# Attention into a gated feed-forward product, one core: weight parts remade from stored raw columns, block sums begun three items ahead, attention in 128-row pieces

## The chip, the cores and the metric

The kernel runs on one core of one Trainium2 chip, as one program. The core has five engines that run side by side and are ordered only by semaphores: PE multiplies matrices, DVE and POOL work element by element, ACT copies, casts and evaluates functions, and SP issues the DMAs, one after the other from one queue, which 16 DMA engines then carry out. PE writes to PSUM, where the tiles lie in eight banks; POOL doesn't read them. The metric is the device time of one execution in microseconds (us), lower is better. The time before is the median of three runs.

## The reference

For each of 8 batches and 8 heads, keys and values are averaged over groups of 8 rows, 576 queries attend to the 72 pooled keys, and the joined heads go through a product of two linear maps and a third:

```python
k_p = k.reshape(B, H, Sp, pool, D).mean(axis=3)      # B, H, S, D = 8, 8, 576, 64; pool 8, Sp = 72
v_p = v.reshape(B, H, Sp, pool, D).mean(axis=3)
scores = scale * np.matmul(q, k_p.transpose(0, 1, 3, 2))
scores = scores - np.max(scores, axis=-1, keepdims=True)
attn = np.exp(scores)
attn = attn / (np.sum(attn, axis=-1, keepdims=True) + 1e-09)
attn_out = np.matmul(attn, v_p)
x = attn_out.transpose(0, 2, 1, 3).reshape(B * S, H * D)          # 4608 x 512
out = ((x @ w_a) * (x @ w_b)) @ w_out                             # 512 -> 1536 -> 512
```

## The kernel before

**High and low parts.** Every factor of a matrix product is split in two: a high part, which is an ACT cast to a shorter format, and a low part, which is what the cast lost, a subtraction on DVE or POOL (`low_part`, L250). A product is then three matmuls, high x high, high x low and low x high. So each split costs one ACT cast and one subtraction, and `either` lets the subtraction go to DVE or to POOL, whichever the planner finds free first.

**Tokens.** The 4608 rows are six pairs of 768, each pair two halves of 384. Attention for a pair must be done before its feed-forward starts. A batch has 576 rows, so that batches end in the middle of halves.

**Attention in pieces.** `chunks_of` cuts each batch by itself into pieces, four of 128 rows and one of 64: 40 pieces. For a piece, `chunk` loads the queries (from the second half on into a `tmp` slot `q`), splits them (`qh`, `ql`), multiplies them with the pooled keys `kdiag` of the piece's batch (matmuls `psc`), subtracts the maximum, takes the exponential, divides by the sum `z`, splits the weights (`pr`, `rem`), transposes them on PE with an identity as moving operand (`ptr`, L836), and copies them out (`turned`, `rest`). Pieces below number `SUMMED` (those of the first two pairs) take scores in three matmuls of 144 columns (L755); the rest in one of 288 and one of 144 (L774, L777). When all pieces of a block (the rows of one batch in one half) are there, `po` matmuls multiply them with the pooled values `vdiag`.

**Feed-forward.** The 1536 hidden columns are 12 groups f of 128, taken in twos j. The first pair is done plainly (`normal`, items "n"): half 0 with j = 0 and 1 alone, then both halves with j = 2 to 5, then half 1 with j = 0 and 1. `ps` matmuls (banks XA, XB, YA, YB) multiply the two weight matrices with the split operands `x`; ACT copies the one product (`h`), DVE multiplies the other onto it, ACT and DVE or POOL split the result (`hh`), and `acc` matmuls multiply it with `w_out`. The other five pairs are items "s" (`block`, one for each j): seven products in the manner of Strassen, with combinations S1 to S4 of the weight blocks (`block_sums`) and T1 to T4 of the operands (`prepare`). The first half of the program until the first "s" item is called the opening here.

**Where weights come from.** In the opening `convert_weights` joins each weight from two 32-bit words (ACT twice, DVE once), as raw columns `raw` for `w_a` and `w_b` and `o` for `w_out`. `split_inner` and `split_outer` split them (`own`, `wo`). Raw columns are stored to DRAM (`kept_raw`, 512 KB for each f); so are the split parts of f 0 to 3 (`kept` from `own`, eight of 512 KB) and the split `w_out` of every f (`kept_o`, 12 of 512 KB). When the plain items come to j = 0 and 1 for the second time, `load_parts` and `load_outer` load these parts again. `block_sums` loads raw columns, makes and stores S1 to S4 (and the split blocks of f from 4 on) two items ahead of their use in pair 1; later pairs load all parts from DRAM.

**Buffers.** `own`, `wo`, `load`, `raw`, `raw2`, `sum` and more share 15 slots of 4 KB for each partition, with a quota for each kind (`QUOTA`); the small tiles share 4 `tmp` slots; `h` has 7 buffers and `hh` 6.

**The order.** No order is written by hand. The class `Machine` plays the whole program through with a cost for each instruction: tasks are generators that ask for an engine or wait for a condition, an engine that is free takes the request with the lowest rank (due times of items and pieces; the products of `inner` come last with 2e4, `outer` with 1e4), and what it takes is issued at once. So each engine's order is fixed when the program is built, and each engine then keeps to it: an instruction that waits holds up all behind it on that engine. Any change of a quota, a due time or a count shifts the order of everything behind.

## Time and profile before

| | |
|---|---|
| median of 3 runs | 1042.36 us (1041.38 to 1043.06) |
| the profiled execution | 1041.39 us |
| its span, first to last instruction | 1039.6 us |
| mean granted TensorE clock | 0.985 |
| PE matmuls, DVE, ACT, POOL instructions | 5424, 1231, 1004, 222 |
| moved by DMA | 230.63 MB, mean 222 GB/s |

The span is 1.8 us shorter than the execution that it belongs to, and that execution lies 1.0 us below the median. A view by stages is the most useful one here, since the opening and the later pairs have different limits. "Busy" is the time in which an engine worked on at least one instruction; matmuls overlap each other, so that a row's mean duration is longer than the distance from one matmul to the next.

### The profile page before, as it was taken

The page shows a single profiled execution, that of the slowest core. Times are in us where ns is not written, and L with a number is a line of the kernel's source. Part 1 is how long each engine was busy: PE and PEld are TensorE (multiplying, and loading weights), DVE is VectorE, ACT ScalarE, POOL GpSimd, SP SyncE. Part 2 cuts the span into 40 slices and gives each one's busy share as a digit, 9 for nine tenths or more (in the row PEclk, how much of TensorE's full clock was granted, in tenths as well). Part 3 has the DMA queues.
Part 4 walks back from the last instruction along what each step waited for, and adds up shares of the span by engine and source line. Part 5 has one row for each costly group of instructions (what it writes and reads, how often), then busy time and mean ns, then how long its engine had stood idle before and what let it go on. Part 6 is the DMA issues. An engine that isn't in the chain of part 4 may idle for free.

```text
span 1039.6 us, 15076 instructions
## 1 busy us (share of the span) xinstructions
PE 992.2 (95%) x5424; PEld 914.4 (88%) x5424; DVE 717.6 (69%) x1231; ACT 470.9 (45%) x1004; POOL 261.8 (25%) x222
## 2 busy tenths in 40 slices
PE   4789799999999999999999999999999999999998
PEld 3678799999889998999998999998899999899997
DVE  7997587477778889757767668669866665634444
ACT  4877686334654455543334354334354334232111
POOL 4353000135444356211116010104210112210000
PEclk9998899999999999999999999999999999999999
DMA  9787874548756676846743768554674645576521
GB/s 332 240 288 247 308 246 158 184 155 304 286 190 224 251 253 258 329 159 242 288 172 133 276 210 315 199 173 170 234 287 172 213 167 182 193 290 212 192 82 61
DMA packets 76426, 230.63 MB, mean 222 GB/s; under 512 B 12288, under 2 KB 12288, under 8 KB 76352
## 3 DMA queue, kind: packets, MB, share of 16 engines
q1 hardware_dynamic: 76352, 229.67, 62.7%
q8 instruction: 43, 0.70, 0.3%
q14 instruction: 31, 0.25, 0.1%
HBM read 184.55 MB, written 45.09 MB: 221 GB/s over the span
## 4 chain that ended last, share of the span: by engine, by line
PE 85%; DVE 6%; ACT 3%; issue 2%; DMA 2%; POOL 1%; POOLq 0%; SPq 0%; ACTq 0%; DVEq 0%
PE acc_s L1195 8%; PE acc_s L1197 8%; PE acc_s L1196 8%; PE psXB L1120 4%; PE psXB L1122 4%; PE psXB L1121 4%; PE psXA L1120 4%; PE psXA L1121 4%; PE psXA L1122 4%; PE psYA L1120 3%; PE psYA L1122 3%; PE psYA L1121 3%; PE psYB L1120 3%; PE psYB L1121 3%; PE psYB L1122 3%; PE ptr L836 3%
## 5 line engine op out<-in xcount | busy, mean ns | idle before, releaser
L1224 DVE TENSOR_TENSOR y<-acc_s,y 128x512 f32<-128x512 f32 x150 | 102.5, 689 | 74.6 <-PE acc_s L1197 73.5
L1195 PE MATMUL acc_s<-wo,hh 128*128 128x512 f32 x360 | 145.8, 405 | 1.9 <-ACT hh L1076 1.9
L1197 PE MATMUL acc_s<-wo,hh 128*128 128x512 f32 x360 | 142.8, 397 | 0.4 <-POOL hh L250 0.4
L1196 PE MATMUL acc_s<-wo,hh 128*128 128x512 f32 x360 | 142.4, 396 | 0.0
L1076 ACT CAST hh<-h 128x384 fp32r<-128x384 f32 x144 | 73.8, 514 | 86.5 <-DVE h L1165 52.0
L250 POOL TENSOR_TENSOR hh<-h,hh 128x384 fp32r<-128x384 f32 x41 | 42.9, 1047 | 271.9 <-ACT hh L1076 235.1
L1147 ACT COPY h<-psXA 128x384 f32<-128x384 f32 x90 | 43.0, 478 | 136.4 <-PE psXA L1122 136.2
L250 DVE TENSOR_TENSOR hh<-h,hh 128x384 fp32r<-128x384 f32 x103 | 67.8, 661 | 27.7 <-ACT hh L1076 26.7
L1197 PEld LDWEIGHTS acc_s<-wo,hh 128*128 128x128 f32 x360 | 67.9, 189 | 17.6 <-POOL hh L250 0.8
L1195 PEld LDWEIGHTS acc_s<-wo,hh 128*128 128x128 f32 x360 | 68.2, 189 | 15.2 <-ACT hh L1076 2.6
L1196 PEld LDWEIGHTS acc_s<-wo,hh 128*128 128x128 f32 x360 | 68.4, 190 | 12.5
L787 ACT ACTIVATE weights<-weights 128x576 f32<-128x576 f32 (+1 forms) x40 | 27.5, 688 | 97.3 <-DVE weights L718 97.3
L796 POOL TENSOR_TENSOR weights<-weights,z 128x576 f32<-128x576 f32 (+1 forms) x24 | 28.4, 1181 | 142.2 <-DVE z L791 132.7
L843 ACT CAST turned<-ptr 128x512 fp32r<-128x512 f32 (+1 forms) x80 | 41.5, 547 | 37.4 <-PE ptr L836 37.3
L1165 DVE TENSOR_TENSOR h<-h,h 128x384 f32<-128x384 f32 x69 | 52.9, 768 | 1.9
L733 DVE TENSOR_REDUCE weights<-psc 128x144 f32<-128x288 f32 (+1 forms) x104 | 43.5, 448 | 12.2 <-PE psc L777 12.2
L1120 PE MATMUL psXB<-xT,load 128*128 128x384 f32 x148 | 50.6, 342 | 0.0
L1120 PE MATMUL psXA<-xT,load 128*128 128x384 f32 x148 | 50.1, 338 | 0.0
L1122 PE MATMUL psXB<-xT,load 128*128 128x384 f32 x148 | 49.7, 336 | 0.0
L1121 PE MATMUL psXB<-xT,load 128*128 128x384 f32 x148 | 49.7, 336 | 0.0
L1121 PE MATMUL psXA<-xT,load 128*128 128x384 f32 x148 | 49.7, 336 | 0.0
L1122 PE MATMUL psXA<-xT,load 128*128 128x384 f32 x148 | 49.7, 336 | 0.0
(322 smaller groups left out, 2885.5 us busy)
## 6 DMA issues: line engine op xcount, KB each, us to landing
load<-kept_S SPq DMA_DIRECT2D x96, 512.0 KB, 4.9
load<-kept SPq DMA_DIRECT2D x86, 512.0 KB, 4.7
wo<-kept_o SPq DMA_DIRECT2D x64, 512.0 KB, 4.7
kept_S<-sum SPq DMA_DIRECT2D x24, 512.0 KB, 3.3
out<-y SPq DMA_DIRECT2D x36, 256.0 KB, 2.2
q<-in_q SPq DMA_DIRECT2D x29, 256.0 KB, 5.0
kraw<-in_k SPq DMA_DIRECT2D x24, 288.0 KB, 4.0
kept_o<-wo SPq DMA_DIRECT2D x12, 512.0 KB, 6.1
```

The lines of the kernel that those rows point to most:

```text
L250: eng.tensor_tensor(out=lo, in0=src, in1=hi.bitcast(F32), op=ALU.subtract)
L733: nc.vector.tensor_reduce(out=s[:n, 2 * g:2 * g + 2, :], in_=pt[:n, :2 * hk].rearrange("p (w h s) -> p h s w", w=2, h=2), axis=AX.X, op=AL ...
L1076: yield on_act(HB, lambda: nc.scalar.copy(e[:, 0], h))
L1120: nc.tensor.matmul(pt, w[:, 0, mat, c], xo[:, 0, kk], start=(opens and kk == 0), stop=False, **more)
L1121: nc.tensor.matmul(pt, w[:, 0, mat, c], xo[:, 1, kk], start=False, stop=False, **more)
L1122: nc.tensor.matmul(pt, w[:, 1, mat, c], xo[:, 0, kk], start=False, stop=(kk == 1), **more)
L1147: yield on_act(HB, lambda: nc.scalar.copy(t, pt))
L1165: yield either(HB, lambda eng: eng.tensor_tensor(out=t, in0=t, in1=a, op=ALU.mult))
L1195: nc.tensor.matmul(pt, e[:, 0, cs], w[:, 0], start=(y == 0), stop=False)
L1196: nc.tensor.matmul(pt, e[:, 0, cs], w[:, 1], start=False, stop=False)
L1197: nc.tensor.matmul(pt, e[:, 1, cs], w[:, 0], start=False, stop=(y == 1))
L1224: yield on_dve(DM, lambda: nc.vector.tensor_tensor(out=acc[row], in0=pt, in1=acc[row], op=ALU.add))
```

## The change

Pieces are now 128 rows each over all 4608 rows, without regard to batches: 36, three to a half. A piece that straddles two batches (number 4, 13, 22 and 31) has its first 64 rows from one and the rest from the other. Its `qh` and `ql` get 64 columns of zeros in the middle (POOL, `clear`), so that two sets of score matmuls, one for each batch's `kdiag`, add up in the same bank. `turned` is now one tile for each half in place of one for each block, and `values_of` multiplies a block's part of it. `SUMMED` becomes 12, still the first two pairs.

Split parts are no longer stored in the opening. `split_again` loads raw columns of f 0 to 3 and splits them again for the plain items that come to j = 0 and 1 a second time. `split_outer` stores raw columns of `w_out` (`kept_ro`, 256 KB) in place of the split ones; `outer_again` loads and splits them again, 4 for those plain items and 12 for pair 1, and stores the latter split (`kept_o`) for the later pairs. `block_sums` begins three items ahead, makes the split blocks of f 0 to 3 too (12 to 18 stores of them), and has 9 `sum` and 4 `raw2` slots; `h` has 6 buffers. New in all are 30 casts, each with its subtraction: 6 of split blocks in `block_sums`, 8 in `split_again` and 16 in `outer_again`.

```diff
-def chunks_of(b):
-    sizes = [128, 128, 128, 128, 64] if b % 2 == 0 else [64, 128, 128, 128, 128]
...
+NCHUNK = B * S // P
+PER_HALF = HB // P
+
+def parts_of(i):
+    out, t = [], i * P
+    while t < (i + 1) * P:
+        n = min((i + 1) * P, (t // S + 1) * S) - t
+        out.append((t // S, t - i * P, n))
+        t += n
     return out
...
-TMP_QUOTA = {"o": 1, "q": 2, "kv": 1}
+TMP_QUOTA = {"o": 2, "q": 2, "kv": 1}
...
-SUMMED = 14
+SUMMED = 4 * PER_HALF
-QUOTA = {"early": 10, "raw": 2, "words": 3, "own": 4, "wo": 4, "load": 7, "raw2": 3, "sum": 6, "T2": 1}
+QUOTA = {"early": 10, "raw": 2, "words": 3, "own": 4, "wo": 4, "load": 7, "raw2": 4, "sum": 9, "T2": 1}
...
-    gates = Slots(sb, "h", 7, {"h": 7})
+    gates = Slots(sb, "h", 6, {"h": 6})
...
-            parts[f, h] = e
-            if f < 2 * LEAD:
-                keep("own", (f, h), e, 1e4 + f)
+            parts[f, h, 0] = e
...
-        tmps.give("o", f)
-        parts["o", f] = e
-        keep("wo", ("o", f), e, 1e4 + f)
+        loaded_o[f] = "wo", f, e
+        def store():
+            kept["raw o", f] = dr.tile([P, 512], F32, name=f"kept_ro_{f}")
+            yield transfer(kept["raw o", f], w, 1 << 18)
+            tmps.give("o", f)
+            mark("kept", "raw o", f)
+        start(due_f[f] + 4, store())
+
+    def split_again():
+        yield lambda: (NF - 1, 1, 0) in parts
+        for f in range(2 * LEAD):
+            yield lambda: ("raw", f) in kept and slots.can("raw2")()
+            r = slots.take("raw2", ("again", f), [P, 2, 512], F32)
+            yield transfer(r.rearrange("p m c -> p (m c)"), kept["raw", f], 1 << 19)
+            for h in range(2):
+                yield slots.can("own")
+                e = slots.take("own", (f, h), e_shape, F32R)
+                src = r[:, :, h * 256:(h + 1) * 256]
+                yield on_act(512, lambda: nc.scalar.copy(e[:, 0], src))
+                yield low(512, e[:, 1], src, e[:, 0])
+                parts[f, h, 1] = e
+            slots.give("raw2", ("again", f))
+        mark("split again")
+
+    def spare_for(kind):
+        return lambda: slots.can(kind)() and (("split again",) in done or len(slots.free) > 3)
+
+    def outer_again():
+        for x in range(NF, NF + 2 * LEAD + NF):
+            f = x - NF if x < NF + 2 * LEAD else x - NF - 2 * LEAD
+            yield until(("kept", "raw o", f))
+            yield lambda: at_item[0] >= NJ - 1 and next_o[0] == x
+            yield spare_for("wo") if x >= NF + 2 * LEAD else slots.can("wo")
+            next_o[0] += 1
+            e = slots.take("wo", x, [P, 2, 512], F32R)
+            yield tmps.can("o")
+            w = tmps.take("o", x, tmp_shape, F32)
+            yield transfer(w, kept["raw o", f], 1 << 18)
+            yield on_act(512, lambda: nc.scalar.copy(e[:, 0], w))
+            yield low(512, e[:, 1], w, e[:, 0])
+            tmps.give("o", x)
+            loaded_o[x] = "wo", x, e
+            if x >= NF + 2 * LEAD:
+                keep("wo", x, e, 1e4 + x, False, ("o", f))
...
-        yield lambda: at_item[0] >= first_s + j - 2
+        yield lambda: at_item[0] >= first_s + j - 3
...
-        if j >= LEAD:
-            yield from split((2 * j, 0), r1[:, :, left])
-            yield from split((2 * j, 1), r1[:, :, right])
+        yield from split((2 * j, 0), r1[:, :, left])
+        yield from split((2 * j, 1), r1[:, :, right])
...
+        gap = P // 2 if len(parts) > 1 else 0
+        qh = sb.tile([P, NK, P + P // 2], F32R, tag="qh", name=f"qh_{i}", bufs=1)
+        ql = sb.tile([P, NK, P + P // 2], F32R, tag="ql", name=f"ql_{i}", bufs=1)
...
+        by_batch = [(b, kdiag[b % 2], slice(x * gap, x * gap + P)) for x, (b, _, _) in enumerate(parts)]
...
-                yield until(("keys", b, g0))
+                yield until(*(("keys", b, g0) for b, _, _ in by_batch))
...
+                        todo = [(qq, w, kd, cs) for _, kd, cs in by_batch for qq, w in ((qh, 0), (qh, 1), (ql, 0))]
```

Three places of the engines' orders, before and after. In these rows the number in a name counts tiles, and shapes are partitions x elements of what is written.

SP, the DMA queue, in the opening; the profile before has these rows issued between 51.9 and 63.2 us. Before:

```order
L247 DMA words_o<-in_wo 128x1024
L247 DMA kept_1_336<-own_22_317 128x1024
L247 DMA words_12_107<-in_wb 128x1024
L247 DMA q_12_617<-in_q 128x512
L247 DMA kept_raw_337<-raw_first 128x1024
L247 DMA kept_o_453<-wo_24_404 128x1024
L247 DMA q_14_687<-in_q 128x512
L247 DMA kept_0_427<-own_23_394 128x1024
L247 DMA words_a<-in_wa 128x1024
```

And now:

```order
L252 DMA kept_raw_360<-raw_first 128x1024
L252 DMA kept_raw_506<-raw_first 128x1024
L252 DMA q_10_548<-in_q 128x512
L252 DMA kept_ro_605<-o_7_331 128x512
L252 DMA words_11_106<-in_wa 128x1024
L252 DMA q_13_642<-in_q 128x512
L252 DMA words_13_108<-in_wo 128x1024
L252 DMA kraw_0_665<-in_k 128x576
L252 DMA kraw_1_666<-in_k 128x576
```

The stores of `own` and the split `wo` between the loads of words are gone; the stores of raw columns stand there alone, those of `w_out` half as wide.

PE, at the first products of the feed-forward, where the first batch ends. Before:

```order
L1047 MATMUL psXB_0_471<-xB_0_385,own_21_274 128x384
L1048 MATMUL psXB_0_471<-xB_0_385,own_21_274 128x384
L836 MATMUL ptr_0_482<-ident,pr_437 128x128 x4
L755 MATMUL psc_0_488<-kdiag_72,qh_423 64x144 x2
L755 MATMUL psc_0_488<-kdiag_72,ql_424 64x144
L755 MATMUL psc_0_488<-kdiag_72,qh_423 64x144 x2
L755 MATMUL psc_0_488<-kdiag_72,ql_424 64x144
L1046 MATMUL psXB_0_471<-xB_0_386,own_22_317 128x384
```

And now, directly behind the matmuls of `psXA` and ahead of those of `psXB`:

```order
L1105 MATMUL psXA_0_443<-xB_0_385,own_22_332 128x384
L819 MATMUL psc_0_463<-kdiag_72,qh_422 128x144 x2
L819 MATMUL psc_0_463<-kdiag_72,ql_423 128x144
L819 MATMUL psc_0_463<-kdiag_73,qh_422 128x144 x2
L819 MATMUL psc_0_463<-kdiag_73,ql_423 128x144
L819 MATMUL psc_0_463<-kdiag_72,qh_422 128x144 x2
L819 MATMUL psc_0_463<-kdiag_72,ql_423 128x144
L819 MATMUL psc_0_463<-kdiag_73,qh_422 128x144 x2
L819 MATMUL psc_0_463<-kdiag_73,ql_423 128x144
```

The piece of 64 rows has become the straddling piece 4, which reads the keys of both batches (`kdiag_72` and `kdiag_73`) and stands ahead of `psXB` as a whole.

ACT, in the plain item that comes to j = 1 a second time, shortly ahead of pair 1. Before:

```order
L456 CAST sum_78_2317<-sums_2303 128x512
L927 CAST xT_1_2313<-xraw_1254 128x768
L927 CAST xT_1_2338<-xraw_1254 128x768
L456 CAST sum_80_2359<-sums_2303 128x512
L1076 CAST hh_21_2383<-h_21_2300 128x384
L1087 COPY h_22_2393<-psYA_1_2364 128x384
```

And now:

```order
L462 CAST own_81_2318<-raw_0_79_2257 128x512
L1133 CAST hh_21_2331<-h_21_2291 128x384
L484 CAST wo_80_2306<-o_31_2307 128x512
L462 CAST own_83_2341<-raw_0_79_2257 128x512
L1144 COPY h_22_2351<-psYA_1_2320 128x384
L507 CAST sum_85_2376<-sums_1966 128x512
```

The casts that remake `own` and `wo` now stand between those that take the products out of PSUM.

More of the change, by code (lines that the diff above doesn't have):

```diff
@@ L86, in __init__ @@
         self.now, self.count = 0.0, 0
-        self.queues = {e: [] for e in ("PE", "DVE", "ACT", "POOL", "SP")}
+        self.queues = {e: [] for e in ("PE", "ACT", "DVE", "POOL", "SP")}
         self.free = dict.fromkeys(self.queues, 0.0)
@@ L429, in split_outer @@
         yield until(("weight", "o", f))
-        yield lambda: slots.can("wo")() and order_o[next_o[0]] == ("own", f)
+        yield lambda: slots.can("wo")() and next_o[0] == f
         next_o[0] += 1
-        e = slots.take("wo", ("own", f), [P, 2, 512], F32R)
+        e = slots.take("wo", f, [P, 2, 512], F32R)
         w = rawt.pop(("o", f))
@@ L440, in block_sums @@
     def block_sums(j):
         left, right = slice(0, 256), slice(256, 512)
-        yield lambda: at_item[0] >= first_s + j - 2
+        yield lambda: at_item[0] >= first_s + j - 3
         r = []
         for f in (2 * j, 2 * j + 1):
-            yield lambda: ("raw", f) in kept and slots.can("raw2")()
+            yield lambda: ("raw", f) in kept and spare_for("raw2")()
             r.append(slots.take("raw2", f, [P, 2, 512], F32))
@@ L453, in split @@
         def split(name, src):
-            yield slots.can("sum")
+            yield spare_for("sum")
             e = slots.take("sum", name, e_shape, F32R)
@@ L768, in chunk @@
             for g in range(NK):
-                yield until(("keys", b, g - g % 2))
+                yield until(*(("keys", b, g - g % 2) for b, _, _ in by_batch))
                 yield bank_there
@@ L819, in chunk @@
         mark("probs", i)
[L821 to L828 removed]
+        half = half_of[i]
+        c0 = (i % PER_HALF) * P
+        if c0 == 0:
+            yield until(("valued", half - 1))
+            both = sb.tile([P, 2, NK, HB], F32R, tag="turned", name=f"turned_{half}", bufs=1)
+            turned[half] = both[:, 0], both[:, 1], sb.tile([P, NG, HB], F32R, tag="rest", name=f"rest_{half}", bufs=1)
         def turn(x, pt):
@@ L852, in chunk, with values_of @@
         mark("turned", i)
-        yield until(*(("placed", c, x) for c in members if c <= i for x in range(3)))
-        if i != members[-1]:
-            return
+        yield until(*(("placed", c, x) for c in range(i - i % PER_HALF, i + 1) for x in range(3)))
+        for j, block in enumerate(blocks):
+            if block[4] == i:
+                yield from values_of(j, rank)
+        if i % PER_HALF == PER_HALF - 1:
+            mark("valued", half)
+            del turned[half]
+    def values_of(j, rank):
+        hf, b, at, total, _ = blocks[j]
+        p = hf // 2
         yield until(("values", b))
-        hf, p = half_of[i], pair_of[i]
-        end = at + n
         if p == 0:
@@ L912, in have @@
     def have(half):
-        return until(*(("x", block_of[i]) for i in range(len(flat)) if half_of[i] == half))
+        return until(*(("x", j) for j, block in enumerate(blocks) if block[0] == half))
     def prepare(p):
@@ L964, in attn_moe_kernel @@
         kind, _, j = item
-        if kind == "n" and not own_parts(item):
-            wanted += [(2 * j + y, h) for y in range(2) for h in range(2)]
-        elif kind == "s":
+        if kind == "s":
             names = {"A11": (2 * j, 0), "A12": (2 * j, 1), "A22": (2 * j + 1, 1)}
             wanted += [names.get(a, (j, a)) for a, *_ in PRODUCTS7]
-        order_o += [("own" if own_parts(item) else "o", 2 * j + y) for y in range(2)]
+        order_o += [("o", 2 * j + y) for y in range(2)]
     loaded, loaded_o = {}, {}
-    second = range(4 * LEAD, 4 * LEAD + 7 * NJ)
     taken = {"i": 0, "o": 0}
@@ L992, in load_outer @@
         for x, name in enumerate(order_o):
-            if name[0] == "own":
+            if x < 2 * (NF + LEAD):
                 continue
-            yield lambda: at_item[0] >= NJ - 1 and name in kept and slots.can("wo")() and next_o[0] == x
+            yield lambda: name in kept and slots.can("wo")() and next_o[0] == x
             next_o[0] += 1
```

174 lines of the change are left out of this document (78 added, 96 removed).

## The prediction

> **What bounds the kernel now.** I read the page first (engines, chain), then busy time cut into stages, then PE's waits in the opening, then the groups of instructions by shape that the change touches.
>
> ```profile
> span 1039.6 us, 15076 instructions
> PE 992.2 (95%) x5424; PEld 914.4 (88%) x5424; DVE 717.6 (69%) x1231; ACT 470.9 (45%) x1004; POOL 261.8 (25%) x222
> PE 85%; DVE 6%; ACT 3%; issue 2%; DMA 2%; POOL 1%; POOLq 0%; SPq 0%; ACTq 0%; DVEq 0%
> ```
>
> PE is the bound over the whole, but 15% of the chain is not PE's. The stages show where. I cut at the first product of f = 6 (130 us), at the first "s" item (247), and then at the first product of each pair (406, 565, 725, 887); columns are window, length, busy time and count of PE, PEld, DVE, ACT and POOL, granted clock, DMA share and GB/s.
>
> ```profile
> 0.00:130.00 130.00, 96.27 (x513) 86.63 (x514) 101.77 (x184) 90.72 (x195) 47.60 (x54) 0.91 0.83 283
> 130.00:247.00 117.00, 116.61 (x643) 108.48 (x642) 80.90 (x131) 59.90 (x117) 20.88 (x13) 1.00 0.59 203
> 247.00:406.00 159.00, 157.24 (x897) 145.74 (x896) 132.73 (x223) 84.96 (x187) 79.02 (x66) 1.00 0.70 250
> 406.00:565.00 159.00, 157.47 (x877) 145.18 (x876) 112.39 (x197) 67.61 (x147) 43.78 (x32) 1.00 0.64 226
> 565.00:725.00 160.00, 157.92 (x867) 146.81 (x866) 113.29 (x201) 66.18 (x145) 24.98 (x21) 0.99 0.61 218
> 725.00:887.00 162.00, 159.60 (x882) 147.09 (x883) 106.30 (x186) 65.83 (x143) 30.07 (x26) 0.99 0.58 204
> ```
>
> From 130 us on PE is idle for 0.4 to 2.4 us in each stage: only fewer or faster matmuls help there, or harm comes from new waits. In the first 130 us PE is idle for 33.7 us, DVE is busy for 101.8 (78%), ACT for 90.7, DMA engines at 0.83. That stage is a race of several engines, DVE the fullest. PE's longest waits in the first 160 us were for others' results:
>
> ```profile
> PE psc L755 <- ACT kdiag L540: 10.4, 2, 8.0
> PE psc L755 <- ACT qh L700: 5.2, 2, 4.7
> PE psXA L1046 <- ACT own L421: 3.3, 1, 3.3
> ```
>
> (us in all, times, longest.) Of these the 8.0 is the start, which the change leaves alone.
>
> **A: the opening up to 130 us.** I counted DVE's instructions in order up to its first multiplication of f = 6: 210 rows before, 192 now. Both have 1152 attention rows behind them there, in ten pieces before (two of 64 rows) and nine now.
>
> ```profile
> L790 DVE TENSOR_REDUCE z<-weights 64x8 f32<-64x584 f32 x8 | 6.0, 746 | 0.7 <-ACT weights L787 0.7
> L733 DVE TENSOR_REDUCE weights<-psc 64x144 f32<-64x288 f32 x24 | 10.1, 440 | 1.8 <-PE psc L777 1.8
> L718 DVE TENSOR_TENSOR weights<-psc,m 64x288 f32<-64x288 f32 x4 | 1.8, 450 | 0.1
> L717 DVE TENSOR_REDUCE m<-psc 64x4 f32<-64x288 f32 x4 | 1.7, 429 | 0.0
> L250 DVE TENSOR_TENSOR own<-raw,own 128x512 fp32r<-128x512 f32 x14 | 10.8, 771 | 6.0 <-ACT own L421 5.9
> L250 DVE TENSOR_TENSOR wo<-o,wo 128x512 fp32r<-128x512 f32 x5 | 4.1, 811 | 0.0
> ```
>
> Gone are 2 `z` (1.5 us), 4 `weights` from PSUM (1.8) and 4 `m` (1.7) of 64 rows, in sum 5.0 us. Five fewer `own` subtractions (3.9) and four more `wo` (3.2) give another 0.6; the five have gone to POOL, which is busy for only 47.6 of these 130 us. So DVE has 5.6 us less. The rest of the difference is work that changes sides of my mark (the third batch's values move behind it, three conversions of words ahead of it), which I leave out. SP and the DMA engines lose much more:
>
> ```profile
> kept_o<-wo SPq DMA_DIRECT2D x12, 512.0 KB, 6.1
> kept<-own SPq DMA_DIRECT2D x8, 512.0 KB, 6.4
> load<-kept SPq DMA_DIRECT2D x86, 512.0 KB, 4.7
> wo<-kept_o SPq DMA_DIRECT2D x64, 512.0 KB, 4.7
> ```
>
> 8 stores of 512 KB go and 12 become 256 KB: 7.3 MB less, 26 us at the stage's 283 GB/s, though some of the twelve are issued after 130 us. A store has no reader in the opening; it costs by holding a slot and by delaying loads behind it. So A lies between nothing (if the 5.6 us was never what PE waited for) and, above, half of PE's idle time that isn't the start, (33.7 - 8.0) / 2 = 13. I take the row that is nearest, DVE's work: **-6**.
>
> **B: the pieces after the opening.** Three more boundaries lose a piece each (the fourth lies within A). A 64-row piece has eight `pr` and two `rem` transposes, like one of 128.
>
> ```profile
> L836 PE MATMUL ptr<-ident,pr 128*128 128x128 f32 x256 | 28.1, 253 | 4.8 <-ACT pr L808 2.7 <-ACT turned L843 1.5 <-DVE pr L250 0.6
> L836 PE MATMUL ptr<-ident,rem 128*96 128x128 f32 x64 | 9.5, 232 | 0.7 <-DVE rem L250 0.4 <-ACT turned L843 0.3
> L836 PE MATMUL ptr<-ident,pr 64*128 64x64 f32 x64 | 7.4, 251 | 0.2 <-ACT turned L843 0.2
> L836 PE MATMUL ptr<-ident,rem 64*96 64x64 f32 x16 | 2.5, 239 | 0.0
> L774 PE MATMUL psc<-kdiag,qh 128*128 128x288 f32 x80 | 22.3, 321 | 0.0
> L774 PE MATMUL psc<-kdiag,qh 128*64 128x288 f32 x24 | 6.2, 295 | 0.0
> ```
>
> Busy time over count is 0.116 and 0.156 us for 64 rows, 0.110 and 0.148 for 128: two small pieces take 2 x (8 x 0.116 + 2 x 0.156) = 2.5 us, one of 128 takes 1.2. Saved: 1.3. The scores save nothing: the straddling piece issues both sets, 8 wide matmuls at 22.3/80 = 0.28 in place of 8 at 6.2/24 = 0.26, so 0.2 is given back and as much again at most for the narrow ones. Net some 1.0 for each boundary, **-3** for three; the ends are -2 and, where the second piece's exchange with other engines costs PE too, -6: a stage with seven pieces (725 to 887) is 2 to 3 us longer than one with six (406 to 565, 565 to 725).
>
> **C: the work put off.** 30 casts and 30 subtractions are new, all between 130 and 406 us.
>
> ```profile
> L421 ACT CAST own<-raw 128x512 fp32r<-128x512 f32 x18 | 11.0, 619 | 0.9 <-PE psYB L1048 0.4 <-DVE raw L408 0.4
> L250 POOL TENSOR_TENSOR own<-raw,own 128x512 fp32r<-128x512 f32 x4 | 5.4, 1360 | 47.9 <-DVE rem L250 28.7 <-ACT own L421 19.2
> ```
>
> ACT gets 30 x 0.62 = 18.6 us. The orders give DVE 16 `wo` more and 3 `own` and 2 `sum` fewer over the whole, some 9 us net, and POOL 11 `own` and 8 `sum` more, 19 x 1.36 = 26 us. What covers it: from 130 to 406 us ACT is busy for 144.9 of 276 us, DVE for 213.6, POOL for 99.9. In front of pair 1's products DVE is at 132.7 of 159 already and PE idles 1.8 us there, no more than at 112.4 of 159 in the next pair (1.5), so the first 20 us of DVE's load cost PE next to nothing. But the casts stand between those that empty PSUM (the order of ACT in the part on the change), and each can hold back a bank by 0.62 us. Bounds: nothing, and the whole of DVE's 9 us. By the row of the neighbouring pair I take **+1**.
>
> DMAs: 14 loads of `load` and 16 of `wo`, 512 KB each, go; 16 of 256 KB, 4 of `raw2` and 6 stores come. That is fewer bytes, at a DMA share of 0.59 to 0.70: nothing. Block sums three items ahead only hold slots longer: nothing, and what they hold up is in C's upper bound. Six `h` buffers in place of seven: the orders of PE in the last pair, where no attention interferes, are equal row for row, so nothing; DVE reading late could make it up to another 2.
>
> **Sum.** -6 - 3 + 1 = -8 from the profiled execution's 1041.4 (span 1039.6 and 1.8 around it) is 1033.4. That execution lies 1.0 under the median, so 1034 is what I expect of a median.
>
> **The rivals** (their times on the median's 1042.4).
>
> *The opening was held by stores and slots, not by DVE.* For it: ACT's conversion of f = 5, for which DVE then sat idle 5.6 us, and PE's wait just behind it.
>
> ```profile
> L408 DVE SCALAR_TENSOR_TENSOR raw<-raw,words_a 128x512 int32<-128x512 int32 x9 | 6.1, 683 | 5.6 <-ACT words_a L399 5.6
> 113.94 0.48 ACT L897 COPY xraw<-po 128x384 f32<-128x384 f32 x1 [0.80 <-PE po L881]
> 114.45 0.33 PE L881 MATMUL po<-rest,vrem 96*128 96x384 f32 x1
> 118.06 0.69 PE L1046 MATMUL psXA<-xB,own 128*128 128x384 f32 x1 [3.27 <-ACT own L421]
> 119.91 0.52 PE L1046 MATMUL psXA<-xB,own 128*128 128x384 f32 x1
> 120.23 0.52 PE L1047 MATMUL psXA<-xB,own 128*128 128x384 f32 x1
> 75.00:100.00 25.00, 22.22 (x122) 20.30 (x122) 18.48 (x37) 17.05 (x39) 10.40 (x10) 0.76 0.71 248
> ```
>
> After that wait PE's matmuls come 0.32 us apart (119.91 to 120.23) and the granted clock of the whole opening is 0.91; a wait that goes takes its slow stretch along. Then A is -13: 1042.4 - 13 - 3 + 1 = 1027. Against it: what ACT waited for there, ahead of the conversion, was PE's `po` (113.94), no store. Chance 0.22.
>
> The Trainium skill, TensorE: Matmul & The Clock Gate, Part 1, says that an idle window of about 3.4 us halves PE's clock until a busy one passes. The row of 3.27 us bears it out. By it the straddling piece cuts the other way: if PE waits that long between `psXA` and `psXB` for the second batch's keys, the products behind run at half speed. It changes the odds of the next rival, not my sum.
>
> *The straddling piece's wait replaces what was saved (no change).* Its scores need the split queries of both halves and both batches' `kdiag`, and stand ahead of `psXB`, with all the first products behind them. The longest such wait before, apart from the start, is 4.7 us (for `qh`); with that A falls to -1: 1042.4 - 1 - 3 + 1 = 1039.4, and up to 1042 if C is also 2 dearer. Against it: the keys' DVE work now stands ahead of `xB`, 14 rows earlier. Chance 0.14.
>
> *DVE becomes the bound of pair 1 (slower).* Place: 247 to 406 us. DVE is the fullest there, POOL at half. If the 9 us of DVE and POOL's slower subtractions (1.36 against 0.77 us each) sit in the path from PSUM to `hh`, PE waits for all of it and for a buffer of `h` besides: C is +9 + 2 and A, by the same queue of splits ahead of the first repeated items, -3. 1042.4 - 3 - 3 + 11 = 1047. It decides once PE's idle time from 130 to 406 grows by over 6 us. Chance 0.14.
>
> That the change doesn't do what it says is excluded by the orders: 36 pieces, no stores of `own`.
>
> **How the numbers follow.** My forecast has 0.5, from 1030 to 1039; the rivals 0.22, 0.14 and 0.14. The range of 8 in 10 takes in the fast rival to 1025 and most of the slow one, to 1046. A measurement of this kernel can tell about 0.2% (2 us) from no change. Faster by more: 0.5 + 0.22 and a third of the second rival (0.03) = 0.75; within: 0.11; slower: 0.14.
>
> **What would show it.** A: the first product of f = 6 near 124 us, not 130, with DVE's busy time up to it near 96. B: 360 transposes `ptr` (the four groups above have 400), and 1 us less in each later stage with a boundary. C: PE's idle time between there and pair 2 not over 4 us more than now, DVE under 145 of the pair's 159. It is wrong if the opening keeps its length (then DVE wasn't its pace), or if PE starts to wait for `h`, `hh` or a repeated `own` behind 130 us.

## The result, and the profile after

Median 1041.87 us before (4 runs, 1041.10 to 1043.06) and 1022.81 us after (4 runs, 1022.28 to 1023.55): ratio 0.982, 95% interval 0.9805 to 0.9835. The gain is 19 us; 8 were forecast, and the range ended at 1025. From the page of the profiled execution after (1022.45 us), its span, busy times and chain:

```profile
span 1020.6 us, 14956 instructions
PE 978.5 (96%) x5380; PEld 907.6 (89%) x5380; DVE 715.7 (70%) x1214; ACT 478.6 (47%) x1002; POOL 271.5 (27%) x233
PE 91%; DVE 5%; ACT 2%; issue 1%; POOLq 0%; DVEq 0%; ACTq 0%
```

PE's share of the chain rises from 85% to 91%; DMA had 2% of it and has gone. The same cut by stages, at the first product of f = 6, of the first "s" item and of pairs 2 to 5 (columns as in the prediction):

```profile
0.00:113.90 113.90, 85.87 (x477) 79.14 (x478) 97.59 (x174) 85.77 (x179) 41.39 (x50) 0.96 0.80 266
113.90:233.30 119.40, 119.40 (x664) 111.83 (x663) 81.36 (x134) 67.55 (x138) 38.12 (x27) 1.00 0.46 160
233.30:390.80 157.50, 154.24 (x868) 143.02 (x866) 139.83 (x228) 90.64 (x191) 74.96 (x62) 1.00 0.78 275
390.80:548.40 157.60, 157.20 (x885) 146.85 (x885) 110.47 (x192) 67.84 (x145) 45.24 (x38) 1.00 0.64 231
548.40:707.10 158.70, 155.93 (x861) 144.91 (x861) 113.33 (x198) 66.81 (x144) 23.88 (x19) 1.00 0.61 220
707.10:867.00 159.90, 157.95 (x876) 146.56 (x877) 102.43 (x179) 63.58 (x134) 31.77 (x28) 0.99 0.59 207
```

In the first row, the opening up to the first product of f = 6, PE is idle for 28.0 us (113.90 - 85.87) where it was 33.7, and its granted clock is 0.96 where it was 0.91. PE's busy time in it falls too, by 10.4 us (96.27 to 85.87). Some 7 of these are the clock's, by an estimate from the two rows: 0.09 x 130.0 = 11.7 us were lost to it before, 0.04 x 113.9 = 4.6 now. So the waits that went took slow stretches along, as the rival on stores and slots had it. DVE's busy time there is 97.6 us, almost the 96 that the prediction wanted, yet the stage ends ten microseconds earlier than it wanted. The first products, in us from the span's start (the run of each part alone, e1 and e2, is told below):

| stage | before | after | e1, weights alone | e2, pieces alone |
|---|---|---|---|---|
| up to the first "s" item | 246.8 | 233.3 (-13.5) | 236.1 (-10.7) | 249.0 (+2.2) |
| pair 1 | 158.8 | 157.5 (-1.3) | 164.8 (+6.0) | 154.0 (-4.8) |
| from pair 2 to the end | 634.0 | 629.8 (-4.2) | 635.8 (+1.8) | 633.1 (-0.9) |
| sum | | -19.0 | -2.9 | -3.5 |

I compare at the first "s" item from here on: at the first product of f = 6 (129.9 and 113.9) PE has less work behind it after than before, and it does some 3 us more in the stage that follows (119.4 us busy, 116.6 before).

Where do the 13.5 us come from? The timelines of SP and ACT show one chain (start, length, engine, instruction). In the changed kernel:

```profile
77.02 0.43 SPq L252 DMA_DIRECT2D kept_raw<-raw  x1
86.89 0.33 SPq L252 DMA_DIRECT2D words<-in_wa  x1
91.73 0.62 ACT L428 CAST own<-raw 128x512 fp32r<-128x512 f32 x1
```

and before:

```profile
104.64 0.42 SPq L247 DMA_DIRECT2D kept_raw<-raw  x1
115.56 0.33 SPq L247 DMA_DIRECT2D words<-in_wa  x1
117.39 1.14 ACT L421 CAST own<-raw 128x512 fp32r<-128x512 f32 x2 [0.39 <-DVE raw L408]
```

`kept_raw<-raw` is the store of the raw columns of f = 3. Only two slots hold such columns (`raw` in `QUOTA`), so f = 5 can't be converted until that store has landed. It is issued 27.6 us earlier, the words of f = 7 follow 28.7 us earlier, and the first cast of f = 5's parts 25.7 us earlier.

### The profile page after: what moved, and what is told of

It reads as the page before. It is cut to its first block, busy times and chain, and to the rows that moved or that the text cites. A ratio compares the mean times of both kernels' runs of the same rounds, so it can differ in the third digit from the quotient of the medians.

```text
span 1020.6 us, 14956 instructions
## 1 busy us (share of the span) xinstructions
PE 978.5 (96%) x5380; PEld 907.6 (89%) x5380; DVE 715.7 (70%) x1214; ACT 478.6 (47%) x1002; POOL 271.5 (27%) x233
## 4 chain that ended last, share of the span: by engine, by line
PE 91%; DVE 5%; ACT 2%; issue 1%; POOLq 0%; DVEq 0%; ACTq 0%
PE acc_s L1248 8%; PE acc_s L1250 8%; PE acc_s L1249 8%; PE psXB L1177 4%; PE psXB L1179 4%; PE psXB L1178 4%; PE psXA L1177 4%; PE psXA L1178 4%; PE psXA L1179 4%; PE psYA L1177 3%; PE psYB L1177 3%; PE psYA L1179 3%; PE psYA L1178 3%; PE psYB L1178 3%; PE psYB L1179 3%; PE ptr L898 2%
## 5 line engine op out<-in xcount | busy, mean ns | idle before, releaser
L255 POOL TENSOR_TENSOR hh<-h,hh 128x384 fp32r<-128x384 f32 x32 | 33.0, 1033 | 267.9 <-ACT hh L1133 240.9
L255 DVE TENSOR_TENSOR hh<-h,hh 128x384 fp32r<-128x384 f32 x112 | 74.5, 670 | 29.0 <-ACT hh L1133 27.8
L860 POOL TENSOR_TENSOR weights<-weights,z 128x576 f32<-128x576 f32 x22 | 27.3, 1242 | 130.6 <-DVE z L855 126.4
L905 ACT CAST turned<-ptr 128x512 fp32r<-128x512 f32 x72 | 39.7, 589 | 29.5 <-PE ptr L898 29.4
L851 ACT ACTIVATE weights<-weights 128x576 f32<-128x576 f32 x36 | 24.8, 688 | 54.1 <-DVE weights L781 53.9
L1216 DVE TENSOR_TENSOR h<-psYA,h 128x384 f32<-128x384 f32 x60 | 33.2, 553 | 23.6 <-PE psYA L1179 22.9
L796 DVE TENSOR_REDUCE weights<-psc 128x144 f32<-128x288 f32 x96 | 40.1, 449 | 13.0 <-PE psc L843 12.8
L1177 PE MATMUL psXB<-xT,load 128*128 128x384 f32 x144 | 49.0, 340 | 0.0
L1177 PE MATMUL psXA<-xT,load 128*128 128x384 f32 x144 | 48.8, 339 | 0.0
L1179 PE MATMUL psXB<-xT,load 128*128 128x384 f32 x144 | 48.4, 336 | 0.0
L1179 PE MATMUL psXA<-xT,load 128*128 128x384 f32 x144 | 48.4, 336 | 0.0
L1178 PE MATMUL psXB<-xT,load 128*128 128x384 f32 x144 | 48.4, 336 | 0.0
```

The source lines that it names most:

```text
L255: eng.tensor_tensor(out=lo, in0=src, in1=hi.bitcast(F32), op=ALU.subtract)
L796: nc.vector.tensor_reduce(out=s[:n, 2 * g:2 * g + 2, :], in_=pt[:n, :2 * hk].rearrange("p (w h s) -> p h s w", w=2, h=2), axis=AX.X, op=AL ...
L1177: nc.tensor.matmul(pt, w[:, 0, mat, c], xo[:, 0, kk], start=(opens and kk == 0), stop=False, **more)
L1178: nc.tensor.matmul(pt, w[:, 0, mat, c], xo[:, 1, kk], start=False, stop=False, **more)
L1179: nc.tensor.matmul(pt, w[:, 1, mat, c], xo[:, 0, kk], start=False, stop=(kk == 1), **more)
```

## The experiments

Theories named in the expectations: **S**, slots held by stores until they land set the opening's pace; **D**, DVE's load does (step A of the prediction); **P**, one plan of the planner is luckier than another; **M**, the stores cost by their bytes; **Q**, they cost by their place in the queue, ahead of the store of raw f = 3; **QS**, S and Q together; **I** and **H**, on pair 1.

### The parts alone

e1_weights_only: the kernel before with the weights' part of the change (also the quotas, six buffers of `h` and the planner's new order of engines), the old pieces.

```diff
-            if f < 2 * LEAD:
-                keep("own", (f, h), e, 1e4 + f)
...
-        keep("wo", ("o", f), e, 1e4 + f)
...
+    def split_again():
...
+    def outer_again():
...
-        yield lambda: at_item[0] >= first_s + j - 2
+        yield lambda: at_item[0] >= first_s + j - 3
```

> The kernel before with the change's handling of weights (raw columns stored and split again, block sums three items ahead, quotas, six h buffers), but with the old pieces of attention. Theory S, slots: in the opening the split parts of f 0 to 3 held their slots until their stores had landed, which held up the raw columns of f = 5 and so PE: the first product of f = 6 comes at 114 to 120 us as in the changed kernel (130 before), and the whole takes 1026 to 1031. Theory D, the prediction's: DVE's load paced the opening, and most of that came off with the piece: the first product of f = 6 stays at 126 to 131, the whole takes 1038 to 1043.

Measured: 1038.33 us, 0.9962 (0.9947 to 0.9976). The first product of f = 6 comes at 116.4 us, as S had it; the time is as D had it, since what the opening gains is lost again behind it.

e2_pieces_only: the kernel before with the 128-row pieces (also six buffers of `h` and the planner's new order of engines); stores, splits and block sums as before.

```diff
-def chunks_of(b):
+def parts_of(i):
...
-SUMMED = 14
+SUMMED = 4 * PER_HALF
```

> The kernel before with the 128-row pieces (and six h buffers and the planner's new tie-break) alone; split parts stored in the opening as before. Theory S: the first product of f = 6 stays at 125 to 131 us and the whole takes 1035 to 1038, what four boundaries save on PE. Theory D: it comes at 121 to 125, the whole takes 1030 to 1034.

Measured: 1037.67 us, 0.9964 (0.995 to 0.9978). The time is as S had it, but the first product of f = 6 comes at 139.4 us, later than either theory's range. Each part alone brings 3 to 4 us, both 19. The table above shows that the opening's gain is the weights', and that alone they give 6 us of it back in pair 1. A part of that comes and goes with the clock: two of e1's ten runs took 1034.4 us at a granted clock of 0.992, the other eight 1037.5 to 1039.6 at 0.988. In e2 the wait on a slot is visible, in the timelines of ACT and DVE:

```profile
117.87 0.66 ACT L405 ACTIVATE raw<-words 128x512 f32<-128x512 f32 x1 [4.87 <-DMA kept_o<-wo]
119.11 0.69 DVE L415 SCALAR_TENSOR_TENSOR raw<-raw,words_a 128x512 int32<-128x512 int32 x1 [6.13 <-ACT words_a L406]
```

ACT's conversion of f = 5 waits 4.87 us for a slot whose split `wo` is still being stored, and DVE waits 6.13 us for ACT.

e3_tie_break: the kernel before with the planner's engines in the changed kernel's order.

```diff
-        self.queues = {e: [] for e in ("PE", "DVE", "ACT", "POOL", "SP")}
+        self.queues = {e: [] for e in ("PE", "ACT", "DVE", "POOL", "SP")}
```

> The kernel before with only the planner's order of engines at equal times changed (ACT asked ahead of DVE), as in the change: no instruction is added or removed. It measures how far the time moves when the plan is merely shuffled. S and D: within 3 us of before. Theory P, that the gain is a luckier plan: it moves by 8 us or more.

Measured: 1041.92 us, 1.0006 (0.9995 to 1.0016). That reshuffle is worth nothing.

### What the stores of the opening cost

e4_own_slots: the kernel before with six slots for own parts.

```diff
-... "own": 4, "wo": 4, "load": 7, "raw2": 3, "sum": 6, "T2": 1}
+... "own": 6, "wo": 4, "load": 7, "raw2": 3, "sum": 6, "T2": 1}
```

> The kernel before with up to six slots for split parts in the opening in place of four; stores and pieces as before. S: the fifth and sixth part needn't wait for a store, f = 5 is converted earlier, the first product of f = 6 comes 4 to 12 us earlier than at 130, the whole takes 1030 to 1038. D: no change, 1040 to 1044.

Measured: 1048.27 us, 1.0068 (1.0043 to 1.0092). S in its simple form missed, and so did D (no change). The timelines say why:

```profile
74.57 0.62 ACT L421 CAST own<-raw 128x512 fp32r<-128x512 f32 x1
...
102.56 0.42 SPq L247 DMA_DIRECT2D kept_raw<-raw  x1
...
123.78 0.64 ACT L421 CAST own<-raw 128x512 fp32r<-128x512 f32 x1
```

The parts of f = 4 are cast at 74.6 us (93.6 before), so their slots did come free. But the store of raw f = 3 still goes out at 102.6 (104.6 before), and f = 5 is later, not earlier.

e5_hold_both, e6_copy_both, e7_hold_outer, e8_hold_inner start from the changed kernel and put the stores back. e5 has both lines below, e7 the second alone, e8 the first alone; in e6 each is a copy from DRAM to DRAM of the same size and rank, for which nothing is held.

```diff
             parts[f, h, 0] = e
+            if f < 2 * LEAD:
+                keep("own", (f, h), e, 1e4 + f, False, ("u%d" % f, h))
...
         loaded_o[f] = "wo", f, e
+        keep("wo", f, e, 1e4 + f, False, ("uo", f))
```

> The changed kernel, with the stores of the opening put back that the change removed: the split inner parts of f = 0 to 3 (8 of 512 KB) and the split outer weights (12 of 512 KB), each holding its slot of the shared pool until its store has landed; nobody reads the copies. Computation on the engines is as in the changed kernel. Theory S (slots held until stores land set the pace of the opening): the first product of f = 6 goes back from 113.9 us to 122 or later, and the time to 1030 or more. Theory M (the stores cost by their bytes, 10.5 MB on the DMA engines): the same here. Theory D (DVE's lighter load set the pace): the first product of f = 6 stays within 2 us of 113.9 and the time within 2 us of 1022.8.

> The changed kernel with the same 20 transfers of 512 KB at the same ranks, but as copies from one DRAM tensor to another, so that no slot is held for them. Theory S: no more than 3 us later than the changed kernel (113.9 us at the first product of f = 6, 1022.8 us in all). Theory M: as late as the run that holds the slots, 122 us or later. Theory D: within 2 us.

> The changed kernel with only the 12 stores of split outer weights put back, slots held. Theory S, from the wait of e2_pieces_only for a slot that such a store held: it has most of the loss of the run that holds both, at least 5 us at the first product of f = 6. Theories M and D: 12 of 20 parts of the loss of both (M), nothing (D).

> The changed kernel with only the 8 stores of split inner parts put back, slots held. Theory S: the smaller part of the loss, 0 to 5 us at the first product of f = 6, with PE's waits for own parts; theory M: 8 of 20 parts of the loss of both; theory D: nothing.

Measured: e5 1034.62 us, 0.9927 (0.9912 to 0.9942); e6 1041.12, 0.9992 (0.9983 to 1.0002); e7 1023.70, 0.9821 (0.9805 to 0.9838); e8 1029.56, 0.988 (0.9865 to 0.9895). D, as the only pace, is out: no arithmetic was added in e5, and 12 of the 19 us are lost; its opening is 12.6 us longer (245.9 against 233.3 at the first "s" item). S's forecast for e6 (3 us) missed by 15. Of e7 and e8 it expected most of the loss in e7, but e7 loses 0.9 us and e8 6.8. At the mark that the expectations name, the first product of f = 6, both are late (126.2 and 123.2 us; 113.9 in the changed kernel), and only e7 makes it up by the first "s" item; so that mark says little of the time. M fits e6 but not e7, where 12 stores, 6.3 MB, cost 0.9 us. e6's timelines separate the two things that a store does:

```profile
85.81 0.62 ACT L428 CAST own<-raw 128x512 fp32r<-128x512 f32 x1
...
114.22 0.43 SPq L252 DMA_DIRECT2D kept_raw<-raw  x1
...
121.64 0.62 ACT L428 CAST own<-raw 128x512 fp32r<-128x512 f32 x1 [5.24 <-DVE raw L415]
```

With no slot held, the parts of f = 4 are as early as in the changed kernel (their second cast at 85.8; there 87.9). But the copies stand in SP's queue ahead of the store of raw f = 3, which goes out at 114.2 in place of 77.0, and f = 5 is late. Hence four runs that only move the raw stores' rank, so that they go ahead: e9_copy_behind is e6 with that edit, e10_hold_behind is e5, e11_before_raw_first the kernel before, e12_after_raw_first the changed kernel.

```diff
-        keep("raw", ("raw", f), rawt[f], 1e4 + f, f > 2)
+        keep("raw", ("raw", f), rawt[f], 9e3 + f, f > 2)
```

> As e6_copy_both (the changed kernel and 20 copies of 512 KB from DRAM to DRAM), but the stores of raw weights rank ahead of the copies (9e3 + f in place of 1e4 + f): the same bytes, another order in the queue. Theory Q (what costs is that the store of raw f = 3, which must land before f = 5 can be converted, stands behind other stores: issued at 77.0 us in the changed kernel, 104.6 before, 114.2 in e6_copy_both): that store is back before 85 us, the first product of f = 6 before 118 us, the time at 1026 or less. Theory M (bytes on the DMA engines, in whatever order): the time stays at 1036 or more.

> As e5_hold_both (20 stores of split parts, slots held), with the stores of raw weights ranked ahead of them. Theory Q: as in the run with the copies, the loss of e5_hold_both (11.8 us) goes down to 3 us or less. Theory S (the slots held by stores, not the order of the queue): the loss stays at 8 us or more, since the stores that hold slots now land later still.

> The kernel before, with the one edit that its stores of raw weights rank ahead of its stores of split parts. Nothing is removed. Theory Q in its simple form: the opening gains most of its 12 us, the time 1032 or less. Theory S, with Q only a part: the store of raw f = 3 waits for its second split, which waits for a slot of own that a store holds, so it stays near 100 us, and the time within 3 us of 1041.9.

> The changed kernel with the same edit: its only other stores of that rank come later, so nothing moves in the opening by theories Q, S and M; within 2 us of 1022.8.

Measured: e9 1027.61 us, 0.9853 (0.9829 to 0.9877); e10 1043.15, 1.001 (1.0 to 1.0019); e11 1046.08, 1.0044 (1.0029 to 1.0059); e12 1023.20, 0.9821 (0.9807 to 0.9836). The edit gives 13.5 us back where nothing is held (e6 to e9). The opening of e9 is whole again; in its profiled execution the 5 us that stay missing are lost in pair 1. They aren't the price of the bytes: one of e9's four runs took 1022.89 us, as the changed kernel does, at a granted clock of 0.995, and the other three 1027.6 to 1028.0 at 0.990. By the median e9 missed Q's 1026, though the store (83.0) and the first product of f = 6 (112.3) came as Q had them; M's 1036 is far off. The edit costs 8.5 us where slots are held (e5 to e10), against Q and as S had it, and 4 us in the kernel before, where Q expected a gain and S no more than 3 us either way. In the changed kernel it does nothing, as expected. From e9's and then from e10's timelines:

```profile
83.02 0.53 SPq L252 DMA_DIRECT2D kept_raw<-raw  x1
...
98.22 0.62 ACT L428 CAST own<-raw 128x512 fp32r<-128x512 f32 x1
```

```profile
90.20 0.62 ACT L428 CAST own<-raw 128x512 fp32r<-128x512 f32 x1
...
99.82 0.42 SPq L252 DMA_DIRECT2D kept_raw<-raw  x1
...
119.05 1.14 ACT L428 CAST own<-raw 128x512 fp32r<-128x512 f32 x2
```

In e10 the stores of split parts now land later, their slots come free later, and f = 3 itself (90.20; 72.5 in the changed kernel) waits for one; its raw columns can't be stored before they are split. A store of a split part thus delays f = 5 by two ways, and moving it in the queue trades one for the other. e13_hold_slots7 relieves both: e10 with seven slots for own parts.

```diff
-... "own": 4, "wo": 4, "load": 7, "raw2": 4, "sum": 9, "T2": 1}
+... "own": 7, "wo": 4, "load": 7, "raw2": 4, "sum": 9, "T2": 1}
```

> As e10_hold_behind (the changed kernel, 20 stores of split parts put back with their slots held, stores of raw weights ranked ahead), with up to 7 slots of the shared pool for own parts in place of 4. Theory QS (a store of a split part costs in two ways: it holds a slot that the next split needs, and it stands ahead of the store of raw f = 3, which f = 5 needs): both are relieved, so the loss of 20.3 us goes down to 6 or less, and the casts of f = 5 come before 105 us (119.0 in e10_hold_behind, 91.7 in the changed kernel). If a third thing costs (the bytes, the DMA engines' time), the loss stays at 10 or more.

Measured: 1026.51 us, 0.9848 (0.9832 to 0.9864).

```profile
82.74 0.49 SPq L252 DMA_DIRECT2D kept_raw<-raw  x1
...
100.72 0.64 ACT L428 CAST own<-raw 128x512 fp32r<-128x512 f32 x1
```

All 20 stores are there, and the first "s" item starts at 231.6 us, earlier than in the changed kernel; the 4 us that stay are lost behind it, and why stays open. What seven slots would do without the stores has no run. The runs on stores, sorted by that start (times of trace rows as above; median of the runs last):

| kernel | first cast of f = 4 | store of raw f = 3 | first cast of f = 5 | first "s" item | median |
|---|---|---|---|---|---|
| e13 | 81.9 | 82.7 | 100.7 | 231.6 | 1026.51 |
| e9 | 82.1 | 83.0 | 98.2 | 232.6 | 1027.61 |
| after | 84.7 | 77.0 | 91.7 | 233.3 | 1022.81 |
| e7 | 82.3 | 87.6 | 99.8 | 233.5 | 1023.70 |
| e8 | 83.5 | 100.0 | 110.4 | 238.9 | 1029.56 |
| e5 | 93.8 | 105.3 | 116.2 | 245.9 | 1034.62 |
| before | 93.6 | 104.6 | 117.4 | 246.8 | 1041.87 |
| e6 | 82.6 | 114.2 | 121.6 | 248.4 | 1041.12 |
| e11 | 101.6 | 101.7 | 116.0 | 249.7 | 1046.08 |
| e10 | 99.8 | 99.8 | 119.0 | 251.2 | 1043.15 |
| e4 | 74.6 | 102.6 | 123.8 | 253.7 | 1048.27 |

Wherever f = 5 is cast by 101 us, the opening is short, and nowhere else. The other runs fit: e2 and e3 cast it at 120.9 and 117.0 us and start the first "s" item at 249.0 and 246.0; e1 and e12 to e18 cast it by 101 and start between 231.6 and 236.1. A late raw store alone spoils the opening (e4, e6). A late slot was never seen alone: where the parts of f = 4 are late, so is the raw store (e5, e10, e11, before). QS holds for the changed kernel; the kernel before with both edits has no run.

### What DVE's load costs

e14_dve_open takes the sum of the exponentials twice in pieces 0 to 8; e15_dve_pair1 has `12 <= i < 19` for the condition. The order of all else stays.

```diff
             nc.vector.tensor_reduce(out=z[:n], in_=wide[:n], axis=AX.X, op=ALU.add)
+            if i < 9:
+                nc.vector.tensor_reduce(out=z[:n], in_=wide[:n], axis=AX.X, op=ALU.add)
```

> The changed kernel with the sum of the exponentials (z) taken twice in pieces 0 to 8: 9 more instructions on DVE in the opening, 9 x 0.755 = 6.8 us by the profile, the planner not told, all else in the same order. Theory D (DVE's load in the opening costs time one for one, as step A of the prediction had it): the first product of f = 6 and the time 5 to 7 us later. Theory QS: DVE has room between what it waits for; 3 us or less.

> The changed kernel with the same doubling in pieces 12 to 18, which are worked on in pair 1's stage: 7 x 0.755 = 5.3 us more on DVE, in the same order. Theory I (pair 1 with the splitting again is near DVE's limit, 140.0 of 157.5 us, so the weights' part gives back 6 us there, and the pieces pay for it by lightening DVE): 3 to 5 us later. Otherwise: 1 us or less.

Measured: e14 1026.29 us, 0.9845 (0.983 to 0.9859); e15 1025.05, 0.983 (0.9814 to 0.9847). Stages by windows, e14's opening and then e15's pair 1:

```profile
0.00:115.50 115.50, 84.98 (x476) 77.44 (x477) 100.74 (x181) 85.15 (x178) 41.84 (x50) 0.96 0.79 262
```

```profile
232.90:392.50 159.60, 154.85 (x867) 142.85 (x866) 145.59 (x234) 90.55 (x191) 76.05 (x62) 1.00 0.77 270
```

The 9 added instructions, 6.8 us by their own durations, make the opening 1.6 us longer (115.5 against 113.9 at the first product of f = 6, and the same at the first "s" item), 0.24 us for each us; 7 of them, 5.3 us, make pair 1 2.1 us longer (159.6 against 157.5), 0.4 for each. These are two executions, and both prices were measured in the changed kernel. D's 5 to 7 us are out for the opening; I is half right for pair 1. By the medians the two cost 3.5 and 2.2 us, between what the theories had. In the profiled executions (spans 1024.2 and 1024.4 us) the other 2.0 and 1.7 us come in later stages, mostly where the granted clock was at half for longer (the last section).

### Plan, buffers and block sums

e16_after_old_tie is the changed kernel with the old order of engines (e3's edit backwards); e17_weights_7h is e1 with seven buffers of `h`; e18_sums_two_ahead is the changed kernel with the block sums' old start.

```diff
-    gates = Slots(sb, "h", 6, {"h": 6})
+    gates = Slots(sb, "h", 7, {"h": 7})
```

```diff
-        yield lambda: at_item[0] >= first_s + j - 3
+        yield lambda: at_item[0] >= first_s + j - 2
```

> The changed kernel with the old order of engines in the planner, ACT and DVE exchanged, which moves instructions throughout. Theory P (a part of the gain is luck of one plan): 1026 or more. Otherwise within 3 us of 1022.8.

> e1_weights_only (the weights' part of the change, pieces as before, 6 buffers of h) with 7 buffers of h. Theory H (with splitting again in pair 1, the buffer of h that was taken away is missing there): pair 1's stage goes from 164.8 us to 160 or less and the time from 1038.3 to 1034 or less. Otherwise, if it is the load of seven pieces and the splitting together: within 2 us of 1038.3, the stage at 163 or more.

> The changed kernel with block sums begun two items ahead, as before, in place of three. By the prediction (block sums three ahead cost and bring nothing) within 2 us of 1022.8. If the early start is what keeps the sums out of pair 1's way: 3 us or more later, all of it between 233 and 391 us.

Measured: e16 1023.72 us, 0.9817 (0.9802 to 0.9831); e17 1038.34, 0.9962 (0.995 to 0.9975), pair 1 again 164.8 us; e18 1033.13, 0.9917 (0.9892 to 0.9943), four runs from 1030.02 to 1035.50. Neither the reshuffle nor the buffer matters, but the early start of the block sums does: 7.6 us by the profiled spans (1028.2 against 1020.6, both at a granted clock of 0.993), 10 by the medians; two of e18's four runs, the two slowest, had a clock of 0.988. The prediction's forecast for it, no change, is out. Pair 1 by windows in e18, e1 and e2:

```profile
231.80:395.80 164.00, 156.79 (x873) 144.80 (x872) 142.72 (x231) 89.36 (x189) 84.36 (x67) 0.99 0.76 271
```

```profile
236.10:400.90 164.80, 159.10 (x884) 145.24 (x883) 138.77 (x235) 93.11 (x200) 81.69 (x66) 0.99 0.75 265
```

```profile
249.00:403.00 154.00, 153.47 (x869) 143.69 (x868) 127.67 (x214) 83.59 (x176) 71.32 (x58) 1.00 0.72 252
```

and PE's longest waits there in e18 (us in all, times, longest):

```profile
PE psXB L1177 <- DVE h L1210: 3.9, 3, 1.9
PE acc_n L1248 <- DVE y L1277: 2.3, 1, 2.3
PE ptr L898 <- ACT turned L905: 1.0, 2, 0.8
```

Three kernels split again in pair 1: the changed one (157.5 us, POOL 75.0), e1 (164.8, POOL 81.7) and e18 (164.0, POOL 84.4), at nearly the same busy time of DVE. The two long ones have 7 to 9 us more on POOL, PE idle for 5.7 and 7.2 us in place of 3.3, and a stretch of half clock each. What splitting again costs shows over pairs 1 and 2 together, since a late pair 1 can be made up in pair 2 (from the first "s" item to the first product of pair 3): 317.8 us before and 324.1 in e1, with the old pieces and the sums early, +6.3; 314.5 in e2 and 323.8 in e18, with the new pieces and the sums late, +9.3; 314.5 in e2 and 315.1 after, with the new pieces and the sums early, +0.6. So it is nearly free only with both. That the two act through POOL is only argued from the busy times; no run changed POOL's work alone. No variant beat the changed kernel.

## Why the prediction was right or wrong

**The bound.** Right: PE over the whole, the opening the one stage with room, 13.5 of 19 us from there.

**A, -6 for DVE's lighter load: this step failed.** "I take the row that is nearest, DVE's work" priced DVE's 5.6 us one for one, and DVE wasn't what the opening waited for. With the pieces alone (e2), and so with DVE's lighter load, the opening is 2.2 us longer, not shorter. By e14 an added us of DVE costs 0.24 us there. What did make the opening faster is the removed stores, by holding no slots and by leaving the queue to the store of raw f = 3: putting them back in the two ways costs 12.6 us of the opening (e5) and 15.1 (e6), and relieving both ways with all stores in place gives it back (e13). That is the upper end of what A allowed, so the bound was right and the choice in it wrong; the rival "held by stores and slots" had the mechanism and -13.

The 5.6 us was also too large. At the mark to which the 210 rows were counted, DVE's multiplication at 146.1 us, eleven pieces lay behind it before, not ten: 1280 rows against 1152. The rows of `z` up to the marks, before and after:

```profile
L790 DVE TENSOR_REDUCE z<-weights x11: 743/753/761, 15.6 to 144.2; 128x8 f32<-128x584 f32 x9, 64x8 f32<-64x584 f32 x2
L854 DVE TENSOR_REDUCE z<-weights x9: 749/760/762, 15.5 to 110.4; 128x8 f32<-128x584 f32 x9
```

For the same rows, a piece of 128 comes for the two of 64 that go. By its rows it costs one `z` of 0.75 us and four reductions and subtractions of some 0.45, 2.6 in all, so that 3.0 of the 5.6 us are left. At e14's price they are worth 0.7 us, by an estimate that carries the price over from the changed kernel.

What spoke against the rival was misread: ACT waited for PE's `po` ahead of the conversion, "no store". But the planner plays the stores' landing through as well, and can put the conversion behind `po` because its slot comes free late; then a missing slot shows as a late place in the order, and only where the plan errs (e2's 4.87 us) as a wait. That this was its reason here follows from how the order is made; no run shows it singly. "A store has no reader in the opening" was true, and that it "costs by holding a slot and by delaying loads behind it" was said; that other stores queue behind it was not asked.

**B, -3 for the pieces.** Right in mechanism, with the size too small. The groups of transposes after count 288 + 72 = 360, as forecast, and take 42.4 us in place of 47.5, 1.3 for each boundary:

```profile
L898 PE MATMUL ptr<-ident,pr 128*128 128x128 f32 x288 | 31.6, 252 | 11.9 <-ACT pr L872 7.0 <-DVE rem L255 2.1 <-DVE weights L781 1.7
L898 PE MATMUL ptr<-ident,rem 128*96 128x128 f32 x72 | 10.8, 234 | 1.1 <-ACT turned L905 0.8 <-DVE rem L255 0.4
```

Behind the first "s" item e2 gains 4.8 + 0.9 = 5.7 us, just inside the bound of -6. In pair 1 most of it is PE's own work, 153.5 us busy against 157.2: eight pieces' transposes were in that stage before (80), six are now (60), where the sum took one less for each boundary. In the kernel before, `SUMMED` = 14 also took in the first piece of the third pair. The rest, some 1 us, is PE's idle time, with DVE at 127.7 us against 132.7.

**C, +1 for the work put off.** Alone it is +6.0 in pair 1 and +1.8 behind it, 7.8 us (e1), near the bound of +9, though some of it comes and goes with the clock. B and C together were put at -2 and came to -5.5 (-1.3 in pair 1, -4.2 behind it), next to e2's -5.7: with the new pieces and the early sums C costs next to nothing. "Block sums three items ahead only hold slots longer: nothing" was wrong by 7 us or more (e18). Six buffers of `h` cost nothing (e17), as said.

**The other rivals.** PE's idle time in pair 1 rose by 1.5 us, to 3.3, and DVE stayed at 139.8, under the 145 that was named, so DVE didn't become the bound. The straddling piece's wait isn't among what e2 lost in the opening: PE's scores wait for `qh` 0.8 us in all there (5.2 before), and its longest wait that is new, 7.3 us of `psXA` for `own`, comes behind the one on `kept_o`.

**The sum.** -13.5 in the opening, A with the opening's share of B in it, and -5.5 for B and C behind it make -19.0. The parts don't add up singly (-2.9 and -3.5): without the weights' part the opening stays held by the stores (e2), and without the new pieces the splitting again costs some 6 us in pairs 1 and 2 (e1). The forecast fell 11 us short of the gain: 7.5 in the opening, by A, and 3.5 behind it, by B and C. Even the fast rival's 1027 was 4 us too slow, since it took B and C at -2 as well.

## What to carry to other kernels

A store that nobody reads soon can still set the pace: it holds its buffer, and it stands in its queue ahead of a store that frees a buffer sooner needed; test the two apart, with a copy that holds nothing and with a change of rank. Where a planner sets the order, look for scarce buffers in what stands late, not only in what waits. Before pricing an engine's work one for one, add a little of it: in two stages of this kernel, with DVE 86 and 89% busy, DVE's work cost 0.24 and 0.4 us per us. And when counting what a change removes, count at marks with the same work behind them.

## What was not expected of the hardware

Stretches at half clock come and go with the same order of instructions. At the start of pair 3 PE has the same gap of 1.75 us in the changed kernel and in e14, but went on at full clock in the one and at half in the other. The timelines of PE, after and then e14:

```profile
551.44 0.44 PE L1177 MATMUL psXB<-xB,load 128*128 128x384 f32 x1 [1.75 <-DVE h L1210]
...
552.60 0.34 PE L1177 MATMUL psYA<-xB,load 128*128 128x384 f32 x1
```

```profile
553.09 0.45 PE L1179 MATMUL psXB<-xB,load 128*128 128x384 f32 x1 [1.76 <-DVE h L1212]
...
554.31 0.52 PE L1179 MATMUL psYA<-xB,load 128*128 128x384 f32 x1
```

The matmul of `psYA` 1.2 us behind the gap takes 0.34 us in one and 0.52 in the other, and the windows from 550 to 560 us show a granted clock of 1.00 and 0.83:

```profile
550.00:560.00 10.00, 8.56 (x44) 7.45 (x45) 8.12 (x15) 3.14 (x8) 0.51 (x1) 1.00 0.18 67
```

```profile
550.00:560.00 10.00, 8.22 (x32) 7.16 (x33) 7.01 (x10) 3.83 (x9) 2.16 (x2) 0.83 0.00 0
```

The Trainium skill, TensorE: Matmul & The Clock Gate, Part 1, says that the window of some 3.4 us runs freely, and these rows agree with that. The idle window of about 3.4 us, by which the prediction went, isn't needed: the gap ahead of the half clock here was about half of that, and the prediction's wait of 3.27 us was under it too. Pair 3's stage is some 1.5 us longer in e13, e14 and e16 than in the changed kernel, each with such a stretch in it, so differences of 2 us between whole times of this series may be no more than that.
